# Sooner loads, stages and output weights in a one-core attention and feed-forward kernel

## The chip, the cores and the metric

The kernel runs on one core of one Trainium2 chip. The metric is the time of one execution in microseconds (us) on the device. Each execution's record also has the mean clock that was granted to the matrix engine, as a share of full speed. Engines are named as in the profile: PE (matrix), PEld (its weight loads), DVE (vector), ACT (scalar), POOL (GpSimd), SP (which only issues DMAs here).

## The reference

Sliding-window attention with four sink keys, on four batches of eight heads, then a gated feed-forward on all tokens (shortened here):

```python
def _attn_ref(q, k, v, n_sink, window):            # B, H, S, D = 4, 8, 768, 64; n_sink 4, window 128
    scores = (1.0 / np.sqrt(D)) * np.matmul(q, k.transpose(0, 1, 3, 2))
    keep = is_sink | in_window                      # key < 4, or 0 <= query - key < 128
    scores = np.where(keep, scores, -1e9)
    a = np.exp(scores - np.max(scores, axis=-1, keepdims=True))
    a = a / (np.sum(a, axis=-1, keepdims=True) + 1e-09)
    return np.matmul(a, v)

def _moe_ref(x, w_gate, w_val, w_out):              # 512 -> 1536 -> 512
    return (np.maximum(x @ w_gate, 0.0) * (x @ w_val)) @ w_out

# x is the attention output as (4 * 768, 512) = (tokens, heads * D); the result is (3072, 512) float32
```

## The kernel before

The program's order on each engine is written by hand, and PE runs its list in that order (in the trace of this kernel nothing else ran on PE in the 3.64 us, up to 82.15 us, in which a matmul waited for wo). The feed-forward is cut into 96 **slots**: per batch two halves of 384 tokens (`g`) times 12 slices of the hidden dimension (`m`). A slot is one `chunk`: four matmuls for the gate, four for the value, a relu on ACT, a product on DVE into `hT`.

```python
def chunk(b, g, m):
    assert all((b, p, g) in ready for p in range(NP)), (b, g)
    x, h = xT[b % 2], hT[b % 2]
    c = slice(CUT * g, CUT * g + CUT)
    gp, vp = G[gvn[0] % 3], G[(gvn[0] + 1) % 3]
    gvn[0] += 2
    for ko in range(KO):
        nc.tensor.matmul(out=gp[:, 0:CUT], lhsT=wg[:, ko, m * 128:(m + 1) * 128], rhs=x[:, ko, c],
                         start=ko == 0, stop=ko == KO - 1)
    gs = gspool.tile([128, CUT], F32, name="gs")
    nc.scalar.activation(gs[:], gp[:, 0:CUT], Act.Relu, bias=0.0, scale=1.0)
    for ko in range(KO):
        nc.tensor.matmul(out=vp[:, 0:CUT], lhsT=wv[:, ko, m * 128:(m + 1) * 128], rhs=x[:, ko, c],
                         start=ko == 0, stop=ko == KO - 1)
    nc.vector.tensor_tensor(h[:, m, c], gs[:], vp[:, 0:CUT], op=Alu.mult)
```

The attention of the *next* batch runs in small stages between the chunks of the present one: T turns keys and queries, S makes scores and exp, V and W multiply with the values, X turns the result into `xT`, which the next batch's chunks read. A digit names the unit (a pair of heads): S21 is group 1 of unit 2. A table says which stage stands behind which slot's chunk, and `prep` says which loads, casts and transfers stand ahead of it:

```python
for s, w in {0: "H1 S04 S02", 1: "H2 S14", 2: "H3 S12", 3: "S24 S22", 4: "S34 S32", 6: "V01", 7: "V11",
             8: "V21", 9: "V31"}.items():
    for y in w.split():
        put(s, y, 0)
for s, w in {12: "T0", 13: "T1", 14: "S00 S01", 15: "S02 S10", 16: "T2 S11", 17: "S12 T3", 18: "W0 S20",
             19: "S21 S22", 20: "W1 S30 X0", 21: "S31 S32", 22: "W2 X1", 23: "W3 X2 F X3"}.items():
    for y in w.split():
        if y == "F":
            plan[s].append((y, 12, 0))
        else:
            put(s, y, 1)
plan[23].append(("F", 6, 0))
for b, sl in ((2, {29: "S00 S01", 31: "S02 S10", 33: "S11 S12", 35: "S20 S21", 36: "W0", 37: "S22 S30",
                   38: "W1", 39: "S31 S32", 41: "W2", 42: "W3"}),
              (3, {48: "S00 S01", 50: "S02 S10", 52: "S11 S12", 54: "S20 S21", 56: "W0", 57: "S22 S30",
                   58: "W1", 59: "S31 S32", 61: "W2", 63: "W3"})):
    for s, w in sl.items():
        for y in w.split():
            put(s, y, b)
prep = [[] for _ in slots]
prep[1] += [("half", 6), ("half", 7), ("w", 6, 8), ("v", 0, 3), ("v", 0, 4), ("w", 8, 10), ("v", 0, 5),
            ("v", 0, 6), ("w", 10, 12)]
prep[8] += [("setup2", 0)]
prep[9] += [("setup3",)]
prep[10] += [("load", 4), ("load", 5), ("load", 6)]
prep[11] += [("kq", 4), ("load", 7), ("lv", 1)]
prep[12] += [("kq", 5)]
prep[13] += [("kq", 6)]
prep[14] += [("kq", 7)]
prep[15] += [("v", 1, j) for j in range(7)]
prep[16] += [("wo",)]
for i, ts in ((8, (14, 18, 19, 23)), (9, (15, 20, 21, 25)), (10, (17, 21, 22, 27)), (11, (19, 22, 23, 29)),
              (12, (30, 33, 35, 37)), (13, (32, 35, 37, 39)), (14, (34, 37, 39, 41)), (15, (36, 39, 41, 46))):
    for t, what in zip(ts, ("rows", "castrows", "td", "turn")):
        prep[t].append((what, i))
    assert at["S", i - NP, 2] < ts[3] < at["S", i, 0] - 1, i
    prep[at["S", i, 0] - 1].append(("sinks", i))
    prep[at["W", i, 0] + 1].append(("xd", i))
    prep[at["W", i, 0] + (3 if i != 11 else 2)].append(("xturn", i))

for b, s0, s1 in ((2, 22, 27), (3, 46, 49)):
    for j in range(7):
        prep[s0 + j].append(("lv", b, j))
        prep[s1 + j].append(("v", b, j))
```

In `prep`, `load`/`lv`/`rows` ask SP for keys and queries, values, and keys and queries in another layout. `kq`, `v` and `castrows` are casts to bf16 on POOL. `wo` asks POOL's DMA queue for the output weights in three pieces. `setup2` makes copies of the masks on DVE, and `setup3` sets constants on POOL. Names in the profile's lines: `kf`, `qf`, `vf` are loaded keys, queries and values, `kn`, `qn`, `vn` their casts, `KQ` turned keys and queries, `ee` the scores after exp, `msk` the masks, `xn` the attention output before it is turned, `ot` an output tile.

Batches 2 and 3 don't use PE to turn their keys: they are cast, written to memory (`td`), and read back by a transposing DMA (`turn`); their attention output goes the same way (`xd`, `xturn`):

```python
def to_dram(u):
    for i, x in enumerate((qn, kn)):
        nc.sync.dma_start(out=kqd[u.i - ND][i * S:i * S + S, :].rearrange("(p n) c -> p (n c)", n=6),
                          in_=x[u.i % 2][:])

def turn(u):
    nc.sync.dma_start(out=KQ[u.i % NT][:, 0:2 * S], in_=kqd[u.i - ND], transpose=True)
# ...
def x_to_dram(u):

    x, d = xn[u.i % 2], xd[u.i - ND]
    for t, r0, n, i in ((0, 0, 128, 4), (1, 128, 124, 3)):
        nc.sync.dma_start(out=d[r0:r0 + 252 * i, :].rearrange("(i r) c -> r i c", r=252)[0:n, :, :],
                          in_=x[0:n, t:t + 2 * i - 1:2, :])

def x_turn(u):
    nc.sync.dma_start(out=xT[u.b % 2][:, u.p, :], in_=xd[u.i - ND][8:8 + S, :], transpose=True)
    for x in range(2):
        ready[u.b, u.p, x] = True
# ...
def load_wo(c):
    nc.gpsimd.dma_start(out=wo[:, 4 * c:4 * c + 4, :],
                        in_=moe_w_out.rearrange("(ko ki) n -> ki ko n", ki=128)[:, 4 * c:4 * c + 4, :])
# ...
def odd_tiles(u, copy):
    e = kE[u.i % NT]
    copy(odd(e)[:, :, 4:128], e[:, 120:876].rearrange("d (i c) -> d i c", c=252)[:, :, 0:124])
    sinks(u, copy)
```

The output matmuls (F, `ffn2`) of a batch wait in a queue, and three are taken per slot from slot 24 on; slot 23 takes 18 at once. What is left runs after the last chunk, in the tail. Before the tail all use one PSUM bank, in the tail three banks in turn:

```python
OP = [[G[3][:]], [G[3][:], PP[0][:, 0, :], PP[1][:, 0, :]]]
opn = [0]
opend = {}
tail = [0]

def ffn2(b, t, m):
    if m == 0:
        ops = OP[tail[0]]
        opn[0] += 1
        opend[b, t] = ops[opn[0] % len(ops)]
    op = opend[b, t]
    nc.tensor.matmul(out=op, lhsT=hT[b % 2][:, m, t * 128:(t + 1) * 128], rhs=wo[:, m, :],
                     start=m == 0, stop=m == FM - 1)
    if m == FM - 1:
        ot = outpool.tile([128, d_model], F32, name="ot")
        nc.scalar.copy(ot[:], op)
        nc.sync.dma_start(out=out[b * S + t * 128:b * S + (t + 1) * 128, :], in_=ot[:])

with tc.manual_schedule():
    nc.vector.memset(idle[:], 0.0)
    spin(7)
# ...
    for _ in range(3 if s > 23 else 0):
        if f2:
            f2.popleft()()
    if b > 0 and m == FM - 1:
        f2 += [lambda b=b, t=t, mm=mm: ffn2(b, t, mm) for t in range(3 * g, 3 * g + 3) for mm in range(FM)]
tail[0] = 1
while f2:
    f2.popleft()()
```

The softmax here doesn't subtract the row's maximum and nothing guards it: scores larger than these inputs give would overflow.

Of the kernel before, what the change touches and what calls it, by code (L numbers as in the profile page):

```python
# [19 lines left out]
def kernel(  # L20
# [45 lines left out]
    wo = const.tile([128, FM, d_model], BF16, name="wo")  # L66
# [377 lines left out]
    with tc.manual_schedule():  # L444
# [62 lines left out]
        plan = [[] for _ in slots]  # L507
        at = {}

        def put(s, y, n):  # L510
            st = (y[0], n * NP + int(y[1]), int(y[2]) if len(y) > 2 else 0)
            at[st] = s
            plan[s].append(st)

        for s, w in {0: "H1 S04 S02", 1: "H2 S14", 2: "H3 S12", 3: "S24 S22", 4: "S34 S32", 6: "V01", 7: "V11",
                     8: "V21", 9: "V31"}.items():
            for y in w.split():
                put(s, y, 0)
        for s, w in {12: "T0", 13: "T1", 14: "S00 S01", 15: "S02 S10", 16: "T2 S11", 17: "S12 T3", 18: "W0 S20",
                     19: "S21 S22", 20: "W1 S30 X0", 21: "S31 S32", 22: "W2 X1", 23: "W3 X2 F X3"}.items():  # L520
            for y in w.split():
                if y == "F":
                    plan[s].append((y, 12, 0))
                else:
                    put(s, y, 1)
        plan[23].append(("F", 6, 0))
        for b, sl in ((2, {29: "S00 S01", 31: "S02 S10", 33: "S11 S12", 35: "S20 S21", 36: "W0", 37: "S22 S30",
                           38: "W1", 39: "S31 S32", 41: "W2", 42: "W3"}),
                      (3, {48: "S00 S01", 50: "S02 S10", 52: "S11 S12", 54: "S20 S21", 56: "W0", 57: "S22 S30",
                           58: "W1", 59: "S31 S32", 61: "W2", 63: "W3"})):  # L530
            for s, w in sl.items():
                for y in w.split():
                    put(s, y, b)
        prep = [[] for _ in slots]
        prep[1] += [("half", 6), ("half", 7), ("w", 6, 8), ("v", 0, 3), ("v", 0, 4), ("w", 8, 10), ("v", 0, 5),
                    ("v", 0, 6), ("w", 10, 12)]
        prep[8] += [("setup2", 0)]
        prep[9] += [("setup3",)]
        prep[10] += [("load", 4), ("load", 5), ("load", 6)]
        prep[11] += [("kq", 4), ("load", 7), ("lv", 1)]  # L540
        prep[12] += [("kq", 5)]
        prep[13] += [("kq", 6)]
        prep[14] += [("kq", 7)]
        prep[15] += [("v", 1, j) for j in range(7)]
        prep[16] += [("wo",)]
        for i, ts in ((8, (14, 18, 19, 23)), (9, (15, 20, 21, 25)), (10, (17, 21, 22, 27)), (11, (19, 22, 23, 29)),
                      (12, (30, 33, 35, 37)), (13, (32, 35, 37, 39)), (14, (34, 37, 39, 41)), (15, (36, 39, 41, 46))):
            for t, what in zip(ts, ("rows", "castrows", "td", "turn")):
                prep[t].append((what, i))
            assert at["S", i - NP, 2] < ts[3] < at["S", i, 0] - 1, i  # L550
            prep[at["S", i, 0] - 1].append(("sinks", i))
            prep[at["W", i, 0] + 1].append(("xd", i))
            prep[at["W", i, 0] + (3 if i != 11 else 2)].append(("xturn", i))

        for b, s0, s1 in ((2, 22, 27), (3, 46, 49)):
            for j in range(7):
                prep[s0 + j].append(("lv", b, j))
                prep[s1 + j].append(("v", b, j))
# [102 lines left out]
```

## Time and profile before

The time was 263.72 us (median of 4 runs, 261.12 to 265.12). The profiled execution has a span of 261.7 us at a mean granted clock of 0.993. Busy time of the engines by stretch of the span, from the view that sums busy time in chosen windows:

| stretch, us | length | PE | DVE | ACT | POOL | DMA, GB/s | what runs |
|---|---|---|---|---|---|---|---|
| 0 to 20.8 | 20.8 | 16.4 | 15.1 | 11.5 | 16.4 | 238 | setup, first attention half |
| 20.8 to 47 | 26.2 | 25.4 | 21.4 | 14.4 | 12.1 | 176 | slots 0 to 12 |
| 47 to 66 | 19.0 | 17.9 | 16.6 | 13.4 | 14.1 | 280 | slots 13 to 20, batch 1's scores |
| 66 to 82.2 | 16.2 | 11.6 | 10.0 | 7.3 | 6.2 | 257 | slots 21 to 23 and the wait for wo |
| 135 to 146 | 11.0 | 8.6 | 2.7 | 2.8 | 0.0 | 171 | end of batch 1, the wait for xT |
| 146 to 200 | 54.0 | 54.0 | 25.9 | 25.2 | 6.4 | 94 | batch 2 |

Read it as: where PE's busy time falls short of the length, PE stood. It stands for 4.6 us in the fourth stretch and 2.4 in the fifth, and there no other engine of the table is full either: what is awaited is on its way by DMA (the mean busy share of the DMA engines is 1.23 and 0.66 in these two stretches). The lines that show what it is are in the prediction below.

### The profile page before, as it was taken

The page shows a single profiled execution, that of the slowest core. Times are in us where ns is not written, and L with a number is a line of the kernel's source. Part 1 is how long each engine was busy: PE and PEld are TensorE (multiplying, and loading weights), DVE is VectorE, ACT ScalarE, POOL GpSimd, SP SyncE. Part 2 cuts the span into 40 slices and gives each one's busy share as a digit, 9 for nine tenths or more (in the row PEclk, how much of TensorE's full clock was granted, in tenths as well). Part 3 has the DMA queues.
Part 4 walks back from the last instruction along what each step waited for, and adds up shares of the span by engine and source line. Part 5 has one row for each costly group of instructions (what it writes and reads, how often), then busy time and mean ns, then how long its engine had stood idle before and what let it go on. Part 6 is the DMA issues. An engine that isn't in the chain of part 4 may idle for free.

```text
span 261.7 us, 5607 instructions
## 1 busy us (share of the span) xinstructions
PE 243.7 (93%) x2219; PEld 141.0 (54%) x2219; DVE 130.7 (50%) x249; ACT 117.0 (45%) x215; POOL 71.7 (27%) x118
## 2 busy tenths in 40 slices
PE   7879998998984999999997999999999999999894
PEld 2455565666662555566653555656555555555441
DVE  7587889798960135666641455655323232232100
ACT  3657922595831337556322675442332333333211
POOL 6795472677523222720500162000000000000000
PEclk9999999999997999999999999999999999999999
DMA  7999986999999899489984971133410111100122
GB/s 191 277 247 193 193 118 186 354 194 289 259 270 248 191 191 268 151 306 202 201 185 108 233 157 40 45 101 104 110 31 37 41 40 43 41 23 19 70 90 80
DMA packets 75570, 40.09 MB, mean 153 GB/s; under 512 B 53528, under 2 KB 71448, under 8 KB 75544
## 3 DMA queue, kind: packets, MB, share of 16 engines
q1 hardware_dynamic: 67080, 34.62, 51.4%
q0 software_dynamic: 7920, 4.72, 12.6%
q10 hardware_dynamic: 544, 0.39, 0.5%
q8 instruction: 17, 0.28, 0.5%
q14 instruction: 9, 0.07, 0.1%
HBM read 28.48 MB, written 11.25 MB: 152 GB/s over the span
## 4 chain that ended last, share of the span: by engine, by line
PE 73%; DMA 12%; ACT 4%; DVE 4%; SPq 2%; issue 2%; POOL 1%; DVEq 0%; ACTq 0%
PE g L437 20%; PE g L417 20%; PE g L422 20%; DMA wo<-in_moe_w_out_dram 7%; PE pp L324 4%; ACT ee L328 3%; PE pp L388 3%; PE pp L437 2%; DMA xd<-xn 2%; DMA vf<-in_v_dram 2%; PE pp L343 1%; DMA xT<-xd 1%; SPq L140 1%; ACT ot L441 1%; PE g L343 1%
## 5 line engine op out<-in xcount | busy, mean ns | idle before, releaser
L424 DVE TENSOR_TENSOR hT<-gs,g 128x384 bf16<-128x384 f32 x96 | 52.8, 551 | 90.8 <-PE g L422 87.5
L420 ACT ACTIVATE gs<-g 128x384 f32<-128x384 f32 x96 | 47.6, 496 | 86.3 <-PE g L417 81.6
L417 PE MATMUL g<-xT,wg 128*128 128x384 bf16 x384 | 78.6, 326 | 3.2 <-DMA xT<-xd 2.4
L422 PE MATMUL g<-xT,wv 128*128 128x384 bf16 x384 | 78.1, 326 | 0.0
L437 PE MATMUL g<-wo,hT 128*128 128x512 bf16 x264 | 70.7, 383 | 5.4 <-DMA wo<-in_moe_w_out_dram 4.4
L417 PEld LDWEIGHTS <-wg 128*128 128x128 bf16 x384 | 36.0, 98 | 33.5 <-issue 2.4
L422 PEld LDWEIGHTS <-wv 128*128 128x128 bf16 x384 | 37.4, 98 | 26.8 <-issue 1.8
L328 ACT ACTIVATE ee<-pp 128x998 bf16<-128x998 f32 (+4 forms) x52 | 44.6, 906 | 14.6 <-PE pp L324 14.6
L437 PEld LDWEIGHTS <-hT 128*128 128x128 bf16 x288 | 26.7, 98 | 31.0 <-issue 7.4
L335 DVE TENSOR_TENSOR ee<-ee,msk 128x838 bf16<-128x838 bf16 (+3 forms) x44 | 32.7, 749 | 12.6 <-ACT ee L328 12.3
L143 POOL CAST vn<-vf 128x512 bf16<-128x512 f32 x28 | 20.0, 723 | 43.7 <-DMA vf<-in_v_dram 43.6
L441 ACT COPY ot<-g 128x512 f32<-128x512 f32 x22 | 12.9, 587 | 26.9 <-PE g L437 26.9
L324 PE MATMUL pp<-KQ 64*128 64x252 bf16 (+7 forms) x320 | 16.4, 223 | 0.9 <-DVE KQ L309 0.4
L324 PEld LDWEIGHTS <-KQ 64*128 64x128 bf16 x320 | 10.8, 94 | 10.0 <-issue 6.8
L388 PEld LDWEIGHTS <-ee 128*128 128x128 bf16 x384 | 13.3, 97 | 2.5 <-issue 1.0
L388 PE MATMUL pp<-vn,ee 128*128 128x65 bf16 x384 | 13.9, 193 | 0.8 <-POOL vn L143 0.8
L180 POOL CAST qn<-qf 128x768 bf16<-128x768 f32 x8 | 7.9, 982 | 23.7 <-DMA kqd<-qn 17.1
L394 DVE TENSOR_TENSOR xn<-pp,rn 128x896 bf16<-128x896 f32 x12 | 13.1, 1092 | 0.4
L180 POOL CAST kn<-kf 128x768 bf16<-128x768 f32 x8 | 8.1, 1010 | 1.7 <-DMA kqd<-kn 0.8
L273 PE MATMUL g<-idle 128*128 128x512 bf16 x15 | 5.7, 530 | 1.3 <-DVE warm L212 1.3
L199 POOL COPY KQ<-KQ 128x372 bf16<-128x372 bf16 x8 | 4.3, 543 | 5.1 <-DMA KQ<-kqd 5.1
L147 POOL CAST kn<-kf 128x768 bf16<-128x768 f32 x4 | 3.3, 828 | 7.5 <-DMA kf<-in_k_dram 6.5
(90 smaller groups left out, 135.4 us busy)
## 6 DMA issues: line engine op xcount, KB each, us to landing
out_dram<-ot SPq DMA_DIRECT2D x24, 256.0 KB
kf<-in_k_dram SPq DMA_DIRECT2D x12, 384.0 KB
qf<-in_q_dram SPq DMA_DIRECT2D x12, 384.0 KB
vf<-in_v_dram SPq DMA_DIRECT2D x12, 256.0 KB
vf<-in_v_dram SPq DMA_DIRECT2D x12, 224.0 KB
kf<-in_k_dram SPq DMA_DIRECT2D x8, 192.0 KB
wg<-in_moe_w_gate_dram POOLq DMA_DIRECT2D x6, 256.0 KB, 8.1
wv<-in_moe_w_val_dram POOLq DMA_DIRECT2D x6, 256.0 KB, 9.3
```

The source lines that it names most:

```text
L143: copy(vn[b % 2][0:rows, j, :, 0:64], vf[0:rows, j, :, :])
L180: nc.gpsimd.tensor_copy(dst[u.i % 2][:].rearrange("p (n h d) -> p h n d", n=6, h=2), src[u.i % NQ][:].rearrange("p (h n d) -> p h n d", n= ...
L324: nc.tensor.matmul(out=ps[:, h, c0:c1], lhsT=kE[t][64 * h:64 * h + 64, x0:x0 + 128], rhs=qT[t][64 * h:64 * h + 64, q0:q0 + c1 - c0], start ...
L328: nc.scalar.activation(x, ps[:, :, b0:n], Act.Exp, bias=0.0, scale=scale)
L335: nc.vector.tensor_tensor(x, x, m.unsqueeze(1).to_broadcast([128, 2, c1 - c0]), op=Alu.mult)
L388: nc.tensor.matmul(out=ps[:, h, 65 * t:65 * t + 65], lhsT=ee[u.i % NE][:, g, h, c0:c0 + 128], rhs=vn[u.b % 2][:, j, 2 * u.p + h, 0:65], st ...
L417: nc.tensor.matmul(out=gp[:, 0:CUT], lhsT=wg[:, ko, m * 128:(m + 1) * 128], rhs=x[:, ko, c], start=ko == 0, stop=ko == KO - 1)
L420: nc.scalar.activation(gs[:], gp[:, 0:CUT], Act.Relu, bias=0.0, scale=1.0)
L422: nc.tensor.matmul(out=vp[:, 0:CUT], lhsT=wv[:, ko, m * 128:(m + 1) * 128], rhs=x[:, ko, c], start=ko == 0, stop=ko == KO - 1)
L424: nc.vector.tensor_tensor(h[:, m, c], gs[:], vp[:, 0:CUT], op=Alu.mult)
L437: nc.tensor.matmul(out=op, lhsT=hT[b % 2][:, m, t * 128:(t + 1) * 128], rhs=wo[:, m, :], start=m == 0, stop=m == FM - 1)
L441: nc.scalar.copy(ot[:], op)
```

## The change

Its intent is to have every operand there when PE comes to it: batch 1's loads are asked for two slots sooner and its stages stand one slot sooner; the output weights are asked for among the value casts instead of behind them; 12 output matmuls leave slot 23; batch 2's scores and outputs stand four slots sooner, and the loads, casts and transfers of batches 2 and 3 mostly one to four. Two V stages of batch 0 stand a slot later. No instruction's work changes.

```diff
--- before.py
+++ after.py
@@ -513,19 +513,16 @@
             plan[s].append(st)
 
         for s, w in {0: "H1 S04 S02", 1: "H2 S14", 2: "H3 S12", 3: "S24 S22", 4: "S34 S32", 6: "V01", 7: "V11",
-                     8: "V21", 9: "V31"}.items():
+                     9: "V21", 10: "V31"}.items():
             for y in w.split():
                 put(s, y, 0)
-        for s, w in {12: "T0", 13: "T1", 14: "S00 S01", 15: "S02 S10", 16: "T2 S11", 17: "S12 T3", 18: "W0 S20",
-                     19: "S21 S22", 20: "W1 S30 X0", 21: "S31 S32", 22: "W2 X1", 23: "W3 X2 F X3"}.items():
+        for s, w in {11: "T0", 12: "T1", 13: "S00 S01", 14: "S02 S10", 15: "T2 S11", 16: "S12 T3", 17: "W0 S20",
+                     18: "S21 S22", 19: "W1 S30 X0", 20: "S31 S32", 21: "W2 X1", 22: "W3 X2", 23: "X3"}.items():
             for y in w.split():
-                if y == "F":
-                    plan[s].append((y, 12, 0))
-                else:
-                    put(s, y, 1)
+                put(s, y, 1)
         plan[23].append(("F", 6, 0))
-        for b, sl in ((2, {29: "S00 S01", 31: "S02 S10", 33: "S11 S12", 35: "S20 S21", 36: "W0", 37: "S22 S30",
-                           38: "W1", 39: "S31 S32", 41: "W2", 42: "W3"}),
+        for b, sl in ((2, {25: "S00 S01", 27: "S02 S10", 29: "S11 S12", 31: "S20 S21", 32: "W0", 33: "S22 S30",
+                           34: "W1", 35: "S31 S32", 37: "W2", 38: "W3"}),
                       (3, {48: "S00 S01", 50: "S02 S10", 52: "S11 S12", 54: "S20 S21", 56: "W0", 57: "S22 S30",
                            58: "W1", 59: "S31 S32", 61: "W2", 63: "W3"})):
             for s, w in sl.items():
@@ -534,25 +531,24 @@
         prep = [[] for _ in slots]
         prep[1] += [("half", 6), ("half", 7), ("w", 6, 8), ("v", 0, 3), ("v", 0, 4), ("w", 8, 10), ("v", 0, 5),
                     ("v", 0, 6), ("w", 10, 12)]
-        prep[8] += [("setup2", 0)]
-        prep[9] += [("setup3",)]
-        prep[10] += [("load", 4), ("load", 5), ("load", 6)]
-        prep[11] += [("kq", 4), ("load", 7), ("lv", 1)]
-        prep[12] += [("kq", 5)]
-        prep[13] += [("kq", 6)]
-        prep[14] += [("kq", 7)]
-        prep[15] += [("v", 1, j) for j in range(7)]
-        prep[16] += [("wo",)]
-        for i, ts in ((8, (14, 18, 19, 23)), (9, (15, 20, 21, 25)), (10, (17, 21, 22, 27)), (11, (19, 22, 23, 29)),
-                      (12, (30, 33, 35, 37)), (13, (32, 35, 37, 39)), (14, (34, 37, 39, 41)), (15, (36, 39, 41, 46))):
+        prep[7] += [("setup3",)]
+        prep[8] += [("load", 4), ("load", 5), ("load", 6)]
+        prep[9] += [("kq", 4), ("load", 7), ("lv", 1)]
+        prep[10] += [("kq", 5)]
+        prep[11] += [("setup2", 0)]
+        prep[12] += [("kq", 6)]
+        prep[13] += [("kq", 7)]
+        prep[14] += [("v", 1, 0), ("v", 1, 1), ("v", 1, 2), ("v", 1, 3), ("wo",), ("v", 1, 4), ("v", 1, 5), ("v", 1, 6)]
+        for i, ts in ((8, (13, 17, 18, 20)), (9, (14, 18, 19, 21)), (10, (15, 20, 21, 23)), (11, (19, 21, 22, 25)),
+                      (12, (28, 31, 33, 36)), (13, (30, 33, 35, 38)), (14, (32, 35, 37, 42)), (15, (34, 37, 39, 43))):
             for t, what in zip(ts, ("rows", "castrows", "td", "turn")):
                 prep[t].append((what, i))
             assert at["S", i - NP, 2] < ts[3] < at["S", i, 0] - 1, i
             prep[at["S", i, 0] - 1].append(("sinks", i))
             prep[at["W", i, 0] + 1].append(("xd", i))
-            prep[at["W", i, 0] + (3 if i != 11 else 2)].append(("xturn", i))
-
-        for b, s0, s1 in ((2, 22, 27), (3, 46, 49)):
+            prep[at["W", i, 0] + 3].append(("xturn", i))
+
+        for b, s0, s1 in ((2, 20, 24), (3, 44, 47)):
             for j in range(7):
                 prep[s0 + j].append(("lv", b, j))
                 prep[s1 + j].append(("v", b, j))
```

## The prediction

> **What bounds the kernel now.** I read the page first, then the matrix engine's waits, then the chain of waits, then the timelines around the two places that the chain names. The page's first part says which engine can be the bound:
>
> ```profile
> PE 243.7 (93%) x2219; PEld 141.0 (54%) x2219; DVE 130.7 (50%) x249; ACT 117.0 (45%) x215; POOL 71.7 (27%) x118
> ```
>
> PE is busy for 243.7 of 261.7 us and no other engine passes 50%. Its instructions are issued in a fixed order and the change adds and removes none (2,219 matmuls in both programs), so time can only be won out of the missing 18 us and out of matmuls that ran slow. PE's waits by what ended them:
>
> ```profile
> PE g L437 <- DMA wo<-in_moe_w_out_dram: 4.4, 2, 3.6
> PE g L417 <- DMA xT<-xd: 2.4, 2, 1.5
> PE g L437 <- ACT ot L441: 0.9, 2, 0.7
> PE pp L388 <- POOL vn L143: 0.8, 2, 0.4
> PE g L417 <- DVE hT L424: 0.7, 1, 0.7
> ```
>
> The columns are total us, times, longest. The two large ones are DMAs: the output weights wo, and the transposed load of batch 2's attention output xT. The rest of the idle time lies in the first 21 us (16.4 of 20.8 us busy) and in the last store after the last matmul at 257.8 us; the change touches neither. The chain of waits (start, us, what) tells where the first comes from:
>
> ```profile
> 56.00 4.80 DMA vf<-in_v_dram
> 60.85 1.23 POOL vn L143 x2
> ...
> 62.76 0.73 POOL wo L208
> 63.49 18.62 DMA wo<-in_moe_w_out_dram
> 82.15 1.86 PE g L437 x4
> ```
>
> POOL asks for wo only behind the last of seven value casts, each of which waits for its load. Asked for at 62.0 to 63.5 us, its three pieces land 10.9, 14.7 and 18.6 us later, and PE stands:
>
> ```profile
> 75.66 1.03 PE L437 MATMUL g<-wo,hT 128*128 128x512 bf16 x4
> 77.48 1.02 PE L437 MATMUL g<-wo,hT 128*128 128x512 bf16 x4 [0.80 <-DMA wo<-in_moe_w_out_dram]
> 82.15 1.86 PE L437 MATMUL g<-wo,hT 128*128 128x512 bf16 x4 [3.64 <-DMA wo<-in_moe_w_out_dram]
> 83.81 0.95 PE L402 MATMUL pp<-ident,xn 128*128 128x128 bf16 x7
> 84.69 1.52 PE L437 MATMUL g<-wo,hT 128*128 128x512 bf16 x6
> ```
>
> After the long wait four matmuls take 1.86 us instead of 1.03: the wait costs more than its length. The loads ahead of all this are asked for by SP at:
>
> ```profile
> 40.71 0.36 SPq L113 DMA_DIRECT2D kf<-in_k_dram  x1
> ...
> 46.16 10.73 SPq L140 DMA_DIRECT2D vf<-in_v_dram  x13
> ```
>
> [...] granted clock 0.84 in 75.66 to 86.04 us, and the slow matmuls follow the 3.64 us wait, not the 0.80 us one. [...] a matmul that waits for wo holds up all later chunks, as at 77.5 to 82.2 us. [...] In 66 to 74 us wo's queue moved 0.99 MB and SP's 1.00 MB: an even share. Asking for wo sooner therefore takes half the rate from what SP has queued then. [...] the trace has 10.9 to 18.6 us, so the measured latencies are used below.
>
> **The change part by part.**
>
> *Batch 1's loads two slots sooner.* A gating copy on ACT holds them; it now stands behind slot 7's relu, which began at 35.5 us, not slot 9's at 40.1. The first load goes out near 36.3 us instead of 40.7. The fourth pair waits for the first pair's casts (3.25 us to landing, about 1 us each), so the value loads start near 42.1 instead of 46.2: 4 us sooner. Nothing is added.
>
> *Batch 0's last two V stages a slot later, T0 and all of batch 1's stages a slot sooner.* DVE does about 2.42 us of work in a V slot against PE's 2.28, and also the 0.6 us of mask copies, so it lags by slot 12 (the 0.67 us wait for hT). The empty slot 8 lets it catch up and the mask copies move behind V31: I count this 0.67 us as gone.
>
> *wo among the casts.* The fourth value piece landed 11.3 us after the value loads began (46.2, 57.5), so now near 53.4; wo is asked for at about 54.1, 54.8 and 55.6. With the old latencies it lands at 65.0, 69.5 and 74.2.
>
> *The 12 output matmuls (F) leave slot 23.* They move to the tail, at the same 0.216 us each: no gain. What PE needs of wo, and when: without F, T0 earlier and the waits gone, I add slot lengths from the old PE timeline (slot 12 at 45.0 us, W0 at 57.9, slot 23's chunk at 72.6, X3 at 73.9, the six F at 74.3). c0 is needed at 74.3, c1 at 75.2, c2 at 76.9: lands with 9, 6 and 3 us to spare. In the old trace 75.66 to 86.04 us took 10.38 us for 18 F and one X (18 x 0.216 + 0.39 = 4.28): 6.1 us to be won, 4.4 of it wait and 1.7 slow clock.
>
> *Batch 2's stages four slots sooner.* xT of batch 2 is then asked for in slot 41 instead of 44 at the latest, ahead of slot 48, some seven slots (about 14 us) before its use. The old wait follows 4.85 us of xd write and 2.65 us of transpose:
>
> ```profile
> 136.79 4.85 DMA xd<-xn
> 141.69 2.65 DMA xT<-xd
> ```
>
> Seven slots hide that: 2.4 us won. *Tail:* 69 instead of 57 output matmuls run after the last chunk, and the PSUM bank order shifts by one group so that one bank isn't used twice running; the 0.67 us wait for ot at 247.3 us should vanish. The final store stays.
>
> Sum: 6.1 + 2.4 + 0.67 + 0.67 = 9.8 us of 263.9.
>
> **The rivals.**
> *(a) A new wait for batch 2's keys.* Its first scores move from slot 29 to 25, by my count from 97.2 to about 78.9 us. The old trace has KQ of batch 2 ready only here:
>
> ```profile
> 84.84 0.50 POOL L199 COPY KQ<-KQ 128x372 bf16<-128x372 bf16 x1 [0.93 <-DMA KQ<-kqd]
> ```
>
> All that comes before it in SP's queue starts 4.4 us sooner, and the transposed load passes one unit's write-out and one value piece (0.65 MB, at 0.26 MB/us 2.5 us); so the copies are done at about 85.5 - 4.4 - 2.5 = 78.6 us. That is as good as no margin. wo's earlier queue takes half the rate from it, but did so before as well. I expect 0 to 3 us of PE wait here, 0.8 on average. It is the main doubt.
> *(b) W0 of batch 1 waits longer for value casts.* Three casts now stand behind 2.2 us of wo issue on POOL: done at about 58.1 us against W0 at 57.9 to 58.4. Before, the wait was 0.8 us. I count no change, plus or minus 1.
> *(c) wo lands too late again.* Its first bytes moved 4 us after the issue; it would need 3 us more than before to hurt.
> *(d) Weights late.* The last gate and value weights stopped moving at about 38 us; the loads now start at 36.3 and share with the last 0.2 MB. They are needed at 40.5 us: about 1 us to spare.
> *(e) Nothing gained, because the DMA total is the bound.* DMA is 90% and more busy up to 97 us; but PE needs only part of that by then, and the share falls to 0.38 after 146 us, so late bytes have room.
>
> **Range and chances.** 9.8 us less 0.8 for (a) and some 0.5 for the others leaves 8.5: 263.9 - 8.5 = 255.4 us. The runs before spread over 261.1 to 265.1, which gives 1.5 us either way; (a) with (b) at its worst costs 4 us more. So 252.5 to 259.5 for 8 in 10. Within 2% begins at 258.6: chance of faster 0.86, same 0.13, slower 0.01.
>
> **What the new profile would show.** Right: no PE wait for wo and none for xT; clock near 1.0 between 70 and 90 us; slot 24's chunk beginning near 75.6 us; wo issued on POOL near 54 us behind four casts; first key loads on SP near 36 us; PE idle down by some 8 us and the page's span near 253. Wrong: a PE wait of over 2 us for KQ near 79 us (rival a), for vn near 58 us (b), or for wo near 75 us (c). A gain under 5 us would mean that DMA congestion moved the wait instead of removing it.

## The result, and the profile after

The changed kernel took 254.12 us (median of 4 runs, 253.84 to 254.67) against 263.72. Ratios here and below are the mean time of one kernel's fast runs over that of the other's fast runs of the same rounds, so not quite the ratio of the medians quoted: 0.967, 95% interval 0.960 to 0.974. The prediction's direction is right, and the time is inside its range. The profiled execution has a span of 252.1 us, 9.6 less, and a granted clock of 1.0.

The page of the changed kernel, and PE's waits (total us, times, longest). Of the lines left out, those of the start-up and one of 0.2 us for xT were there before, too:

```profile
PE 241.7 (96%) x2219; PEld 140.1 (56%) x2219; DVE 131.6 (52%) x249; ACT 117.1 (46%) x215; POOL 69.6 (28%) x118
```

```profile
PE pp L324 <- DVE xn L394: 1.5, 1, 1.5
...
PE pp L324 <- DVE KQ L287: 0.4, 1, 0.4
PE g L437 <- ACT ot L441: 0.2, 1, 0.2
...
PE pp L324 <- POOL KQ L195: 0.2, 1, 0.2
...
```

No wait for wo, for the transposed load of xT or for vn is left. A new one has come, 1.45 us for xn. The timelines of PE, of POOL, and of PE again around that wait:

```profile
75.23 0.55 PE L402 MATMUL pp<-ident,xn 128*128 128x128 bf16 x7
75.62 1.46 PE L437 MATMUL g<-wo,hT 128*128 128x512 bf16 x6
76.91 0.81 PE L417 MATMUL g<-xT,wg 128*128 128x384 bf16 x4
```

```profile
53.07 0.83 POOL L143 CAST vn<-vf 128x512 bf16<-128x512 f32 x1 [0.27 <-DMA vf<-in_v_dram]
53.84 2.23 POOL L208 DMA_DIRECT2D wo<-in_moe_w_out_dram  x3
56.04 2.30 POOL L143 CAST vn<-vf 128x512 bf16<-128x512 f32 x3
58.30 1.18 POOL L180 CAST qn<-qf 128x768 bf16<-128x768 f32 x1
59.43 0.82 POOL L180 CAST kn<-kf 128x768 bf16<-128x768 f32 x1
60.20 0.82 POOL L180 CAST qn<-qf 128x768 bf16<-128x768 f32 x1
...
78.45 0.50 POOL L199 COPY KQ<-KQ 128x372 bf16<-128x372 bf16 x1 [0.51 <-DMA KQ<-kqd]
```

```profile
63.02 0.62 PE L324 MATMUL pp<-KQ 64*128 64x252 bf16 x14 [1.45 <-DVE xn L394]
```

wo is asked for at 53.8 us behind four casts, and F runs at full rate at 75.62 with nothing awaited. Slot 24's chunk begins at 76.91 instead of 86.04. The 9.6 us split by the same marks in both traces: 9.13 us up to slot 24, of which 2.6 are the 12 F that only moved (12 x 0.216), so 6.5; 2.2 us from there to the value matmuls of slot 48 (144.55 and 133.20 us), where xT was awaited; and the rest, 117.15 against 118.90 us, is 1.75 longer for the 2.6 us of F that came back, so 0.85 shorter. 6.5 + 2.2 + 0.85 = 9.6. In the tail the 0.67 us wait for ot is gone: the group of 12 that began at 247.32 us in the same bank as the nine before it begins, in the changed kernel, in another bank and at once.

### The profile page after: what moved, and what is told of

The parts are those of the page before. It is cut to its first block, busy times and chain, and to the rows that moved or that the text cites.

```text
span 252.1 us, 5608 instructions
## 1 busy us (share of the span) xinstructions
PE 241.7 (96%) x2219; PEld 140.1 (56%) x2219; DVE 131.6 (52%) x249; ACT 117.1 (46%) x215; POOL 69.6 (28%) x118
## 4 chain that ended last, share of the span: by engine, by line
PE 82%; DVE 7%; ACT 4%; DMA 2%; issue 2%; POOL 0%; SPq 0%; ACTq 0%; POOLq 0%; DVEq 0%
PE g L417 22%; PE g L422 22%; PE g L437 21%; PE pp L324 5%; PE pp L388 4%; PE pp L437 3%; ACT ee L328 3%; DMA kf<-in_k_dram 1%; DMA vf<-in_v_dram 1%; DVE hT L424 1%; DVE KQ L199 1%; PE pp L343 1%; PE g L343 1%; PE g L301 1%; PE pp L320 1%
## 5 line engine op out<-in xcount | busy, mean ns | idle before, releaser
L437 PE MATMUL g<-wo,hT 128*128 128x512 bf16 x252 | 66.7, 379 | 0.3 <-ACT ot L441 0.2
L335 DVE TENSOR_TENSOR ee<-ee,msk 128x838 bf16<-128x838 bf16 (+3 forms) x44 | 31.1, 713 | 12.3 <-ACT ee L328 11.7
L441 ACT COPY ot<-g 128x512 f32<-128x512 f32 x21 | 12.3, 587 | 19.0 <-PE g L437 19.0
L324 PE MATMUL pp<-KQ 64*128 64x252 bf16 (+7 forms) x320 | 16.7, 223 | 2.3 <-DVE xn L394 1.5
L180 POOL CAST qn<-qf 128x768 bf16<-128x768 f32 x8 | 7.0, 872 | 18.5 <-DMA kqd<-qn 14.2
L180 POOL CAST kn<-kf 128x768 bf16<-128x768 f32 x8 | 7.2, 895 | 3.6 <-DMA kf<-in_k_dram 3.2
L437 PE MATMUL pp<-wo,hT 128*128 128x512 bf16 x36 | 8.1, 379 | 0.0
L308 ACT COPY KQ<-g 128x384 bf16<-128x384 bf16 (+3 forms) x15 | 3.9, 347 | 2.4 <-PE g L301 2.3
```

The costliest lines, as they stand in the source:

```text
L180: nc.gpsimd.tensor_copy(dst[u.i % 2][:].rearrange("p (n h d) -> p h n d", n=6, h=2), src[u.i % NQ][:].rearrange("p (h n d) -> p h n d", n= ...
L324: nc.tensor.matmul(out=ps[:, h, c0:c1], lhsT=kE[t][64 * h:64 * h + 64, x0:x0 + 128], rhs=qT[t][64 * h:64 * h + 64, q0:q0 + c1 - c0], start ...
L335: nc.vector.tensor_tensor(x, x, m.unsqueeze(1).to_broadcast([128, 2, c1 - c0]), op=Alu.mult)
```

## The experiments

Twelve runs were made (eleven new kernels and the changed one once more), each on one chip with runs of the kernel before. Medians are over all runs; one of e1's four was slow and is left out of its ratio. The runs of one call compare best; between calls a kernel differs by up to 1 us (the changed kernel itself: 254.1 and, later on another chip, 255.1).

| run | start from | edit | median us | ratio to before (95%) | span, clock of the profile |
|---|---|---|---|---|---|
| e1_wo_alone | before | wo among the casts | 261.28 | 0.994 (0.980 to 1.008) | 260.3, 0.993 |
| e2_wo_last | after | wo behind the casts | 254.05 | 0.970 (0.959 to 0.982) | 252.0, 1.0 |
| e3_b2_late | after | batches 2, 3 as before | 257.99 | 0.984 (0.971 to 0.998) | 255.6, 0.993 |
| e8_loads_late | after | batch 1's loads as before | 257.87 | 0.985 (0.973 to 0.996) | 255.7, 1.0 |
| e4_b2_alone | before | batches 2, 3 sooner | 259.46 | 0.984 (0.979 to 0.990) | 256.9, 1.0 |
| e5_spin | before | idle matmuls in the wait for wo | 263.47 | 1.000 (0.994 to 1.006) | 263.6, 0.994 |
| e10_v_early | after | V stages as before | 254.34 | 0.963 (0.958 to 0.968) | 251.2, 0.999 |
| e9_f12_back | after | 12 F back in slot 23 | 255.16 | 0.968 (0.963 to 0.972) | 252.9, 0.997 |
| after_again | after | none | 255.14 | 0.969 (0.964 to 0.974) | 254.5, 1.0 |
| e6_odd_act | after | one copy to ACT | 254.41 | 0.966 (0.962 to 0.971) | 252.7, 0.998 |
| e7_odd_act_masks | after | the same, masks in slot 8 | 253.34 | 0.965 (0.959 to 0.971) | 251.8, 0.998 |
| e11_odd_act_two | after | two copies to ACT, masks in slot 8 | 254.24 | 0.966 (0.960 to 0.972) | 253.4, 0.998 |

### Which part ends the wait for wo: e1 and e2

e1, from the kernel before:

```diff
-        prep[15] += [("v", 1, j) for j in range(7)]
-        prep[16] += [("wo",)]
+        prep[15] += [("v", 1, j) for j in range(4)] + [("wo",)] + [("v", 1, j) for j in range(4, 7)]
```

> The kernel before with one part of the change: the output weights are asked for after the fourth value cast, not after the seventh. Theory (latency counts from the issue): POOL issues them near 58.1, 58.8 and 59.6 us instead of 62.0 to 63.5; with the old 10.9, 14.7 and 18.6 us to landing they are there at about 69, 74 and 78. PE needs the third piece at 77.4, so the wait falls from 4.4 us to about 1, no slow clock follows, and the time falls by about 4.5 us, to some 259. The xT wait of 2.4 us stays. Rival (the DMA queues are the bound, the order of asking does not matter): the third piece lands near 82 again and the time falls by less than 1 us.

The wait for wo went entirely: from the first F to slot 24's chunk took 4.7 us (79.94 to 84.66) instead of 10.4. But the time fell by 1.5 us on the ratio, with an interval that includes no change, so the expected 4.5 were missed. And the wait went mostly because PE came late. wo was asked for at 61.1 us, not 58.1, and its last piece landed at 81.54 us, only 0.6 sooner than before (82.11), while PE came to the first F 4.3 us later than before (79.94 against 75.66). Of these, 1.9 us had been lost by slot 12, 1.6 of them in waits for the weights wv at 22 to 35 us, ahead of all that the edit touches and absent in the profile of before; the loads of batch 1 started 2.0 us later with them. PE's timeline of e1 shows where most of the rest went:

```profile
63.99 0.25 PE L388 MATMUL pp<-vn,ee 128*128 128x65 bf16 x3 [1.30 <-POOL vn L143]
...
66.15 1.46 PE L417 MATMUL g<-xT,wg 128*128 128x384 bf16 x4
67.40 1.49 PE L422 MATMUL g<-xT,wv 128*128 128x384 bf16 x4
...
79.94 2.75 PE L437 MATMUL g<-wo,hT 128*128 128x512 bf16 x12
```

Issuing wo took POOL 2.23 us ahead of the last three casts, W0 now waited 1.93 us for them (0.77 before), and behind that wait eight matmuls took 2.7 us (66.15 to 68.82) instead of 1.4: the granted clock was 0.67 in 66 to 71 us, against 1.00 in the kernel before. In this profile, asking for wo among the casts moved part of the wait to W0.

e2, from the changed kernel, moves `("wo",)` back behind `("v", 1, 6)` in the same list.

> The changed kernel with this one part undone: the output weights are asked for after all seven value casts. Theory (two cures for one wait, each nearly enough): with the loads four us sooner the casts end near 56.6 us, so the weights are asked for at about 57 to 58.6 and land at 68, 73 and 78, against a need at 75.6, 76.5 and 78.2: a wait of 0 to 0.5 us, time within 0.5 us of the changed kernel (254.1). Rival (the place among the casts is what brings the gain): a wait of 3 us or more comes back and the time rises by 4 us or more.

Measured: 254.05 us, no wait for wo, although its issue began 2.9 us later (56.7 us; landing after 11.2, 15.2 and 19.0 us). So with the loads early, the place of wo in the list is worth nothing that can be measured. Of the theory of two cures for one wait, e2 shows one half: the early loads (and F out of slot 23) are enough. The other half e1 does not show, since its PE came late. e8 below comes nearer: with the first key load at 40.7 us as before, wo among the casts was asked for at 58.0 us and landed by 78.72, 3.4 us sooner than before, and was not awaited; but there the 12 F had left slot 23, too, so what the place alone does stays open.

### What the sooner loads carry: e8

```diff
-        prep[8] += [("load", 4), ("load", 5), ("load", 6)]
-        prep[9] += [("kq", 4), ("load", 7), ("lv", 1)]
-        prep[10] += [("kq", 5)]
-        prep[11] += [("setup2", 0)]
+        prep[10] += [("load", 4), ("load", 5), ("load", 6)]
+        prep[11] += [("kq", 4), ("load", 7), ("lv", 1), ("kq", 5), ("setup2", 0)]
```

> The changed kernel with only the batch 1 loads put back to slots 10 and 11. Theory: first key load near 39.8 us instead of 36.3, 3.5 us later; PE waits for the casts of the first unit (about 0.5 us), for the last value cast at W0 (cast at about 61.8 against a need near 59.5: 2 us or more) and perhaps for the keys of batch 2 at slot 25 (1 to 2 us, since the old margin is 1.2 us). Time up by 3 to 5 us, to 257 to 259. Rival (the loads' slot is slack, the other parts give the gain): time within 1 us of 254.1.

Up by 3.8 us against e2, which stands in for the changed kernel (257.87 and 254.05 in medians), as expected, in small pieces: 0.9 us at W0 (2 expected), 1.8 us for batch 2's keys in three places, and lesser ones ahead. wo, asked for at 58.0 us, was not awaited. The loads' slot is not slack: some two fifths of the gain stand on it, though none of it as a wait for wo.

### Batch 2's stages: e3 and e4

e3 puts the table row of batch 2 and, for batches 2 and 3, the `rows`, `castrows`, `td`, `turn` slots, `lv`, `v` and `xturn` of the changed kernel back to the old ones (all lines of the diff from `for b, sl in` on that concern them); e4 puts the new ones into the kernel before.

> The changed kernel with the stages, loads and casts of batches 2 and 3 put back to their old slots. Theory: the wait for xT at slot 48 comes back, 2.4 us, and the time rises by 2 to 2.6 us (to about 256.5); no wait for wo. Rival (the xT wait vanished because DMA is less crowded by then, not because of the slots): no wait for xT, no change in time.

The time rose by 3.7 us on the ratios (0.984 and 0.970 for e2; 3.5 in the spans of the profiles), more than the 2 to 2.6 expected. The wait for xT came back, 2.7 us in all, and the clock fell behind it (0.93 in 130 to 155 us, 1.00 in the changed kernel; timeline of PE in e3):

```profile
132.80 0.32 PE L417 MATMUL g<-xT,wg 128*128 128x384 bf16 x1 [0.96 <-DMA xT<-xd]
134.83 0.32 PE L417 MATMUL g<-xT,wg 128*128 128x384 bf16 x1 [1.71 <-DMA xT<-xd]
...
136.42 1.46 PE L437 MATMUL g<-wo,hT 128*128 128x512 bf16 x3
137.67 1.49 PE L417 MATMUL g<-xT,wg 128*128 128x384 bf16 x4
```

From 136.42 to 139.89 us eleven matmuls took 3.47 us for 1.95 at full rate (3 x 0.65): 1.5 us lost. 2.7 + 1.5 is the cost in its place; PE had come to slot 24 0.65 us sooner than in e2 (75.58 against 76.23 us).

> The kernel before with one part of the change: batches 2 and 3 have their loads, stages and outputs in the new slots; batch 1, the output weights and the 12 F are as before. Theory: the xT wait of 2.4 us goes, the waits for wo (4.4 us, plus 1.7 of slow clock) stay, and since PE comes to slot 25 only at 88 us the keys of batch 2 (old copies done at 85.5 us) cause no new wait: time down by 2 to 2.5 us, to about 261.3. Rival (batch 2's loads crowd the output weights out): the wait for wo grows by over 1 us and eats the gain.

The time fell by 4.2 us on the ratio, twice what was expected. xT was not awaited any more (2.4), and also the wait for wo shrank to one:

```profile
80.61 1.02 PE L437 MATMUL g<-wo,hT 128*128 128x512 bf16 x4 [1.74 <-DMA wo<-in_moe_w_out_dram]
```

PE came to F 1.3 us later, held by a DVE wait of 1.09 us, and the last piece landed 1.5 us sooner, at 80.6 us (16.7 us after its issue, 18.6 before); behind this wait of 1.74 us the clock did not fall (1.00 in 76 to 90 us). Slot 24 began at 83.60 instead of 86.04 us. All three pieces landed 1.5 us sooner, so what sped them up came ahead of the first. Why is open: from 66 to 78 us both queues moved what they had moved before, within 0.05 MB per 4 us. The rival, that batch 2's loads crowd wo out, is refuted.

### The slow clock by itself: e5

In the kernel before, 14 matmuls without use stand ahead of the ninth of the 12 F:

```diff
-                    for _ in range(i):
+                    for n in range(i):
+                        if i == 12 and n == 8:
+                            spin(14, 0)
                         f2.popleft()()
```

> The kernel before with 14 idle matmuls of 128x512 (14 x 0.216 = 3.0 us of PE work without use) put where PE stands still for the third piece of the output weights[...]. Theory[...]: the weights land at the same time, but the matmuls after the wait run at full rate, 4 in about 1.0 us instead of 1.86: the granted clock stays at 1.0 and the time falls by 1.2 to 1.7 us although work was added. Rival (the slow matmuls come from traffic on the memory, not from the clock): they stay slow, no change in time, or a loss.

PE's timeline of e5, at the wait for wo and at the wait for xT:

```profile
78.30 3.19 PE L273 MATMUL g<-idle 128*128 128x512 bf16 x14
82.14 1.02 PE L437 MATMUL g<-wo,hT 128*128 128x512 bf16 x4 [0.65 <-DMA wo<-in_moe_w_out_dram]
...
142.96 0.32 PE L417 MATMUL g<-xT,wg 128*128 128x384 bf16 x1 [2.19 <-DMA xT<-xd]
144.89 0.48 PE L417 MATMUL g<-xT,wg 128*128 128x384 bf16 x1 [1.61 <-DMA xT<-xd]
145.17 1.48 PE L422 MATMUL g<-xT,wv 128*128 128x384 bf16 x4
```

At its place the theory held: wo landed as late as before (82.14 us), but the four matmuls behind it took 1.02 us instead of 1.86, and the stretch from the first F to slot 24 took 8.95 us instead of 10.38, with more work in it, and the granted clock in 76 to 90 us was 1.00 instead of 0.88. So the slow matmuls were the clock, not traffic. The time did not move at all (ratio 1.000). PE was 0.91 us ahead at batch 2's last W (128.93 against 129.84 us), but the DMAs that bring xT were not: the piece for the second of these matmuls landed at 144.9 us, 144.4 before. The wait for xT grew from 2.4 to 3.8 us and took the gain back, and behind this longer wait the clock fell in its turn (0.93 in 130 to 155 us, 1.00 before), and the four matmuls at 145.17 us took 1.48 us instead of 0.81. Two waits in a row on DMAs must be cured together.

The clock goes with the scatter of the kernel before, too. The one fall to half in its profile lasted 3.41 us (81.44 to 84.85 us, granted clock 0.50), which takes 0.0065 from the mean clock of 261.7 us: 0.993 is one such fall, and 0.987 would be two. Of its 22 fast runs, the four with a granted clock above 0.996 took 261.1 us on average, the ten around 0.993 took 263.5, the eight below took 264.1. In the changed kernel's ten timed runs the clock was 0.997 to 1.0.

### The V stages and the 12 F: e10 and e9

e10 has `8: "V21", 9: "V31"` in the changed kernel; e9 has `23: "F X3"` with the 12 F of before.

> The changed kernel with the last two V stages of batch 0 back in slots 8 and 9. Theory: DVE lags again by slot 12, and a wait of about 0.7 us for hT or xT comes back near 43 to 45 us; time up by 0 to 0.7 us, as later waits on DVE may swallow it. Rival (the place of the V stages does not matter, T0 and the rest sets DVE's lag): no wait, no change.

The rival was right: no wait for hT or xT came back at 40 to 46 us, the time is that of the changed kernel or a little under it. 

> The changed kernel with the 12 output matmuls back in slot 23, ahead of X3. Theory: wo is there in time (landed by 74.5 us, needed from 74 to 76), so PE just does these matmuls 2.6 us sooner; the tail has 57 instead of 69 matmuls and there the same bank is used twice running, so the 0.67 us wait for ot comes back: time up by 0.3 to 0.7 us. Rival (moving these matmuls out of slot 23 was needed to keep PE from waiting for wo): a wait for wo of 1 us or more comes back.

No wait for wo came back, and the waits for ot rose from 0.2 to 1.2 us in three places, 0.67 us of it in the tail. Against e10 (it differs from the changed kernel only by its V stages), the time is 0.8 us higher in medians; the ratio intervals touch, so the sign is likely and the size is not settled.

### The new wait on DVE: after_again, e6, e7 and e11

What held xn in the changed kernel is in DVE's timeline. DVE was busy without a gap from 53.7 to 64.0 us, and a copy that takes 0.27 us in the kernel before (first line) took 1.57 us (second line):

```profile
57.99 0.27 DVE L199 COPY KQ<-KQ 128x372 bf16<-128x372 bf16 x1
```

```profile
59.59 1.57 DVE L199 COPY KQ<-KQ 128x372 bf16<-128x372 bf16 x1
```

It ended as POOL's row of casts (58.30 to 61.02 us, above) ended. The edits: e6 gives the copy of the last unit to ACT, e11 those of the last two; e7 and e11 also move `("setup2", 0)` to slot 8.

```diff
-        odd_tiles(u, nc.vector.tensor_copy)
+        odd_tiles(u, nc.scalar.copy if u.i == 7 else nc.vector.tensor_copy)     # e11: u.i >= 6
```

> The changed kernel once more, on the chip of the next two runs, to compare with them: 254.1 us, with the new 1.45 us wait of batch 1's second unit of scores for DVE near 63 us.

> The changed kernel with one unit's odd key tiles (the last unit of batch 1) copied by ACT instead of DVE. In the changed kernel DVE took 1.57 us for this copy at 59.6 us, 0.27 us at best, while POOL was casting, and PE then waited 1.45 us for xn behind it. ACT was idle from 58.6 to 60.1. Theory (DVE is the bound of 44 to 62 us, and this copy is the part that collides): xn is done 1.4 to 1.7 us sooner, the wait falls to under 0.3 us and the time by 1.0 to 1.5 us. Rival (the wait is set by W0's own end on PE or by ACT): ACT's copy delays the exp of the next scores, wait and time stay.

> As the run before, and the three mask copies on DVE put from slot 11 into slot 8, where no V stage stands. In the changed kernel they took 1.1 us at 45.2 us, just ahead of the first unit's query copy, and PE waited 0.43 us for a query copy at 49.7. Theory: DVE takes them in its free time near 39 us, the 0.43 us wait goes: 0.2 to 0.5 us under the run before, 1.3 to 1.9 us under the changed kernel. Rival: DVE catches up anyway by 49 us, no difference between these two runs.

In e6 and e7 PE's wait did not fall but moved: 1.9 us for the query copy one stage earlier. The copy of the unit before had come under the casts, with 2.45 us in e6 and in e7

```profile
55.65 3.01 DVE L199 COPY KQ<-KQ 128x372 bf16<-128x372 bf16 x1
```

while POOL cast from 56.0 to 58.5 us. The masks' move did what it should (the 0.4 to 1.0 us wait near 50 us is gone in e7 and e11), but the medians of e6 and e7, 254.41 and 253.34, do not differ clearly.

> The changed kernel with the odd key tiles of the last two units of batch 1 copied by ACT, and the mask copies in slot 8. With one unit's copy on ACT the wait did not go: the copy of the unit before, still on DVE, took 2.45 and 3.01 us instead of 0.28, ending as POOL's row of casts ended, and PE waited 1.9 us for the query copy behind it. Theory (a DVE copy from SBUF to SBUF stands as long as POOL casts go on): with both copies on ACT no such copy is left on DVE between 52 and 64 us, PE's waits for DVE there fall under 0.4 us, the span falls by 1.3 to 1.9 us against the run with one copy on ACT (251.8), to about 250.2, and the time to about 251.8. Rival (DVE is simply too busy there, or ACT becomes the bound of it): a wait of over 1 us stays, for DVE or for exp on ACT.

That theory fell as well. With both copies on ACT, the mask products on DVE, 0.68 and 0.60 us in the changed kernel at best, took their place, and PE waited 1.64 us (DVE and POOL in e11):

```profile
56.44 1.51 DVE L335 TENSOR_TENSOR ee<-ee,msk 128x1014 bf16<-128x1014 bf16 x1 [0.52 <-ACT ee L328]
57.87 0.54 DVE L424 TENSOR_TENSOR hT<-gs,g 128x384 bf16<-128x384 f32 x1
58.33 2.08 DVE L335 TENSOR_TENSOR ee<-ee,msk 128x838 bf16<-128x838 bf16 x1
```

```profile
56.20 2.21 POOL L143 CAST vn<-vf 128x512 bf16<-128x512 f32 x3
58.37 0.82 POOL L180 CAST qn<-qf 128x768 bf16<-128x768 f32 x1
59.14 0.82 POOL L180 CAST kn<-kf 128x768 bf16<-128x768 f32 x1
```

The product at 58.33 us lasts until 60.4, a little past the casts' end at 59.96. The one between them, which reads PSUM, takes its usual 0.54 us. So it is not one copy: copies and mask products of DVE, which have their operands in SBUF, can both stand when they meet the casts (1.57 us for 0.27, and 2.08 for 0.60). They do not always: at 56.64 us in the changed kernel a mask product took its usual 0.68 us and POOL's cast of the same moment took 1.15 instead of some 0.62, and in e2, with wo asked for behind the casts, the copy at 59.50 us took 0.41 us and PE waited 0.21 us there. So where they met, mostly one side stood: DVE with 2.08 us for 0.60, or POOL with 1.15 us for 0.62. What decides which, and how long it can stand, these traces do not show: the copy of 3.01 us in e7 stood beside four casts, and it began while POOL was still issuing wo's DMAs. No kernel here beats the changed one clearly. Breaking up the casts, or giving some to ACT, was not tried.

## Why the prediction was right

- **PE is the bound; only waits and slow matmuls can be won.** Right. 2,219 matmuls in both traces, and PE's share went from 93% to 96%.
- **The loads start near 36.3 us and the values near 42.1.** Right: SP asked at 36.30 and 41.79 us.
- **wo is asked for at 54.1, 54.8, 55.6 and lands in time; 6.1 us.** Right in time and size: 53.8 to 55.3 us, to landing 11.2, 15.2 and 19.2 us. The pieces had 10.6, 6.7 and 4.1 us to spare (9, 6 and 3 said). What it did not say is that the same gain comes without this part (e2); alone, this part brought no gain clear of noise (e1). One reading beside it was off, and nothing rests on it. The even share of wo's queue and SP's in 66 to 74 us is one of bytes written; wo is cast on the way, from float32 to bf16, and read at twice that, its queue had 74.9% of the DMA engines' time against 39.9%, and in 74 to 82 us it moved 0.58 MB against 1.56. And the 10.9 to 18.6 us are those of three DMAs in a row: they landed 4.6 us apart.
- **The slow clock costs 1.7 us.** That the slow matmuls are the clock was shown at their place by e5 (four matmuls in 1.02 us instead of 1.86, granted clock 1.00 instead of 0.88). The size is a little too large: it was taken as 6.1 less the 4.4 of wait. The clock was at half from 81.44 to 84.85 us, and PE worked from 82.15, so 2.70 us at half rate cost 1.35. The other 0.3 is the end of the last matmul before each of the two waits (1.03 us for 4 x 0.216).
- **Seven slots hide the xT wait; 2.4 us.** Right. e3 shows that the wait comes back with the old slots, and that it can cost 1.5 us more through the clock.
- **The tail's 0.67 us.** Right in the trace, with the bank order as the reason; e9 brings the wait back.
- **The empty slot 8 lets DVE catch up; 0.67 us.** The wait went, but this step's reason failed: e10 puts the V stages back and the wait stays away. Left as reasons are T0 ahead of slot 12's chunk and the masks out of slot 8. e7 and e11 put the masks back into slot 8, with the V stages late, and the wait stays away there, too, so T0's sooner place is the likelier one; no run puts both the V stages and the masks back.
- **Rival (a), batch 2's keys, 0.8 us on average.** The copies were done at 79.1 us (78.6 said) and PE came for them at 80.3 (78.9 said): no wait in this execution. In after_again and e11 PE waited 1.57 and 1.56 us for the next unit's keys, and in the changed kernel's own profile 0.18 us for the third unit's, so the margin is as small as was feared, one or two units further on.
- **Rival (b), the value casts.** Cast by 58.34 us, used from 58.54: no wait at all.
- **Rivals (c) to (e).** wo was in time (above). Late weights: none in the profiles of before and after; eight of the others have waits for wv of 0.2 to 1.6 us at 22 to 35 us, and e1 with 1.6 and e4 with 0.3 have the loads in their old slots, so sooner loads are not needed for them. The DMA total was not the bound: the span fell by 9.6 us.
- **Slot 24 at 75.6 us.** It was 76.91. The 1.3 us are the wait for DVE at 63.0 us, which no step had: the sum looked at when POOL's casts end, and not at what they do to DVE. It was covered by chance, by the 1.3 us set aside for (a) and the rest and by the vn wait of 0.77 us that went.

Sum: 9.8 worked out, 8.5 forecast, 9.6 in the profiles and medians, 8.7 by the ratio. The 1.5 us either way that the range allows for scatter was read from a spread of 4.0 us, which is 2.0 either way.

## What to carry to other kernels

When the busiest engine runs a fixed list, look for its few long waits and follow each back to the instruction that *asked* for the operand; what stands ahead of that request in its queue is the cure. Undo each part of a change by itself, try each alone, and when a wait is gone, look whether the operand came sooner or the engine later: here the wait for wo stays away when wo's place is put back, the sooner place alone brought no gain clear of noise, and a microsecond won ahead of a second DMA wait was handed back there. After moving work sooner on one engine, check which other engine's operations it now runs beside.

## What else the traces show

- The length of one gap on PE does not tell whether the clock falls. In e1 gaps of 1.30, 0.30 and 0.33 us within 2.4 us had a fall behind them (granted clock 0.67 in 66 to 71 us), in e3 gaps of 0.96 and 1.71 us (0.93 in 130 to 155 us). In the kernel before nearly the same two gaps, 0.85 and 1.53 us, left the clock alone (1.00 in 135 to 146 us), and so did one of 1.74 us in e4 (1.00 in 76 to 90 us). In the clock records of the packed traces of before and after, full speed begins at 6.34 and 7.03 us, and what falls there are begin a whole number of times 3.413 us later: 22 times for the fall at 81.44 us, 75 and 72 times for those behind the last matmul. Cut on this grid, PE's busy time in the 3.41 us ahead of the fall at 81.44 us was 0.48 us; in every other such stretch of these two traces up to the last matmul it was 1.90 us or more, and no fall followed. The two gaps of before fell into two stretches, with 2.54 and 1.90 us busy. That it is the busy share of a fixed stretch that counts, and not the length of one gap, is the estimate from these numbers.
- The three pieces of wo, asked for one behind the other beside SP's loads, took 8.9 to 19.4 us from issue to landing in all 13 kernels: the first 8.9 to 11.5, each next one 4.4 to 5.4 more from landing to landing.
- Where copies or mask products of DVE stand beside POOL's casts, the profile shows operations that grow (0.27 to 3.01 us for one copy on DVE) with no wait, so that the engine looks busy.
